# Scores of two heads on the two halves of the PE array, and an integer add in the weight decoder, in an attention and MLP kernel

## The chip, the cores and the metric

The kernel runs on one core of one Trainium2 chip. The metric is the device time of one execution in microseconds (us); lower is better. Five engines with a queue each work side by side: TensorE (PE, with its weight loads PEld), VectorE (DVE), ScalarE (ACT), GpSimd (POOL) and SyncE (SP), which here only issues DMAs. Each engine takes its instructions in the order in which the program has them.

## The reference: what is computed

```python
# q, k, v: 4 batches, 8 heads, 768 rows, head size 64; n_global = 8, n_local = 96
scores = q @ k.T / sqrt(64) + bias          # bias = -slope[head] * distance
scores = where(first 8 columns or the last 96 rows back, scores, -1e9)
x = softmax(scores) @ v                     # heads joined: 3072 tokens x 512
h = x @ w_in                                # 512 -> 2048, weights in float64
out = (h * clip(h + 3, 0, 6) / 6) @ w_out   # 2048 -> 512
```

## The kernel before, in words

The 3072 tokens are eight blocks of 384 (three tiles `t` of 128). A *pair* `n` is two neighbouring heads of one block, four pairs a block. For each pair and tile, `scores` multiplies the queries with a band of 232 keys (128 in the first tile of a batch), a DVE instruction adds the distances and takes the least ("weighing", L785), ACT takes the exponential and its sum (L789), `sum_up` and `normalize` divide (POOL for all pairs but the first), and `values` multiplies with V; `put_x` splits the result into a high and a low part, `xh` (ACT, L151) and `xl` (DVE, L152).

The first twelve pairs (`EARLY`, three blocks) go in plain float32: the normalized weights are turned by PE (`turn`, L815 and L817) and copied out by ACT (L819). For these, the queries of a pair lie in SBUF as two columns of 128 partitions, each with the other head's half zeroed, so that one matmul over all 128 partitions, with the keys of both heads stacked, gives the scores of one head. The other twenty pairs run in the fp32r format with split operands (`split`, L751 to L758) beside the MLP, in units of work that `attention` lays out.

The MLP runs in steps `f` of 128 hidden columns, sixteen a block: `first` (12 matmuls into `hp`, L165), the gate on ACT and DVE (`g`, L176 and L177), its high and low part (`gh`, `gl`), and `second` (9 matmuls into `acc`, L197). Weights arrive as float64 words in 32 chunks, two to a step. `decode` turns a chunk into two fp32r parts: ACT takes the magnitude (`wz`, L370), then DVE clamps (L389), shifts (L402), puts the sign back (L408), makes the exponent's value (L417), scales the low word by it (L392), adds (L406), and after ACT's rounding copy (L414) takes the rest (L399): seven DVE instructions of 128x512 a chunk. `fetch` loads a chunk into one of two buffers (`wst`).

Order: in the early stage a loop over `n` emits the scores of pair `n+2`, the turning of pair `n`, the sums of pair `n+1` and the values of pair `n-1`. A planner strews decoding steps and MLP steps between: `work(pe, dve)` books costs for PE and DVE, and while PE's account is ahead, the next decoding step is emitted; `decoded_to` forces steps that an MLP step needs. `LEAD` is the DVE account's start, `FIRST` the number of MLP steps of block 0 that go out within the early stage (after that, blocks 0 and 1 alternate, still with decoding). From pair 8 on (`self.more` false) the PSUM banks `acc` and `hp` belong to the MLP. PE, SP and POOL keep the order of emission; a scheduler places DVE's and ACT's instructions. `WAKE` idle matmuls open the program.

## Time and profile before

| | us |
|---|---|
| median of 3 runs | 675.01 (674.8 to 675.87) |
| the profiled execution, its own time | 674.91 |
| its span, first to last instruction | 673.0 |
| PE busy | 657.1 (98%) |
| DVE, ACT, POOL busy | 438.6, 282.9, 192.6 |

In a row of the timeline stand the start, the duration, the engine, the line, the operation, the tiles (written <- read), shapes and a count, and in brackets the time that the engine had been idle before and who ended that. Instructions of an engine overlap a little, so the distance from one start to the next (its *pitch*) is what an instruction costs the engine. A float32 matmul stands as two records.

### The profile page before, as it was taken

The numbers are of one execution on the slowest core, as the hardware profiler recorded it, in microseconds if no ns is written. First come the engines' busy times: TensorE is split into PE (matmuls) and PEld (weight loads), VectorE is DVE, ScalarE is ACT, GpSimd is POOL, SyncE is SP. The second block draws the span as 40 slices with busy tenths as digits, with TensorE's granted clock in tenths as the row PEclk, the third lists the DMA queues.
The fourth block names the chain that finished last, engine by engine and source line by source line (L and its number), as shares of the span: only waits on it lengthen the run. The fifth ranks groups of instructions, "written<-read, shape, count | busy, mean of one in ns | idle before, by whom it ended". The sixth has DMA issues, their size and how long they took to land.

```text
span 673.0 us, 11339 instructions
## 1 busy us (share of the span) xinstructions
PE 657.1 (98%) x3913; PEld 590.5 (88%) x3913; DVE 438.6 (65%) x1186; ACT 282.9 (42%) x744; POOL 192.6 (29%) x354
## 2 busy tenths in 40 slices
PE   7999899999999999999999999999999999999996
PEld 6788789999999889899989999899989999989995
DVE  8799899999975666457653676447762676422221
ACT  6899655554446333144333433143331443231111
POOL 2855400000000443233340343315431343302110
PEclk9999999999999999999999999999999999999999
DMA  8677432333303446524654367534555255510001
GB/s 255 176 230 242 146 124 100 121 110 110 97 29 133 131 135 181 158 94 132 165 140 119 103 172 189 147 94 126 138 160 141 79 150 142 141 47 2 1 1 52
DMA packets 62611, 84.33 MB, mean 125 GB/s; under 512 B 8784, under 2 KB 48720, under 8 KB 62544
## 3 DMA queue, kind: packets, MB, share of 16 engines
q1 hardware_dynamic: 62256, 83.25, 43.1%
q8 instruction: 33, 0.54, 0.3%
q14 instruction: 34, 0.28, 0.1%
q10 hardware_dynamic: 288, 0.26, 0.1%
HBM read 62.52 MB, written 20.97 MB: 124 GB/s over the span
## 4 chain that ended last, share of the span: by engine, by line
PE 84%; DMA 5%; ACT 4%; DVE 3%; issue 1%; POOL 1%; SPq 0%; POOLq 0%; ACTq 0%
PE hp L165 38%; PE acc L197 32%; DMA wst<-w 5%; ACT n L789 2%; PE sp L778 2%; PE xp L859 2%; PE tp L859 2%; PE sp L197 2%; PE tp L197 2%; PE xp L197 2%; PE tp L778 2%; POOL n L807 1%; ACT pt L819 1%; DVE n L785 1%; ACT wz L370 0%
## 5 line engine op out<-in xcount | busy, mean ns | idle before, releaser
L176 ACT ACTIVATE g<-hp,small 128x384 f32<-128x384 f32 x127 | 73.9, 582 | 256.0 <-PE hp L165 226.1
L165 PE MATMUL hp<-xh,w1h 128*128 128x384 f32 x512 | 174.0, 340 | 0.0
L165 PE MATMUL hp<-xh,w1l 128*128 128x384 f32 x512 | 172.8, 337 | 0.0
L165 PE MATMUL hp<-xl,w1h 128*128 128x384 f32 x512 | 171.9, 336 | 0.0
L183 POOL TENSOR_SCALAR gh<-g 128x384 fp32r<-128x384 f32 x96 | 57.8, 602 | 295.1 <-DVE g L177 265.2
L197 PE MATMUL acc<-w2h,gl 128*128 128x512 f32 x336 | 132.9, 396 | 0.1
L197 PE MATMUL acc<-w2l,gh 128*128 128x512 f32 x336 | 132.8, 395 | 0.0
L197 PE MATMUL acc<-w2h,gh 128*128 128x512 f32 x336 | 132.2, 393 | 0.0
L807 POOL TENSOR_SCALAR n<-n,sums 128x232 f32<-128x232 f32 (+1 forms) x186 | 104.9, 581 | 52.6 <-DVE sums L798 47.0
L177 DVE SCALAR_TENSOR_TENSOR g<-g,hp 128x384 f32<-128x384 f32 x128 | 70.2, 549 | 76.0 <-ACT g L176 75.4
L789 ACT ACTIVATE n<-n,least 128x232 f32<-128x232 f32 (+1 forms) x192 | 89.7, 471 | 40.3 <-DVE least L785 39.6
L190 DVE TENSOR_TENSOR gl<-g,gh 128x384 fp32r<-128x384 f32 x128 | 73.2, 572 | 45.7 <-POOL gh L183 44.0
L165 PEld LDWEIGHTS hp<-xh,w1h 128*128 128x128 f32 x512 | 96.3, 188 | 5.5 <-issue 1.5
L165 PEld LDWEIGHTS hp<-xl,w1h 128*128 128x128 f32 x512 | 96.2, 188 | 3.9
L165 PEld LDWEIGHTS hp<-xh,w1l 128*128 128x128 f32 x512 | 96.0, 188 | 0.0
L197 PEld LDWEIGHTS acc<-w2l,gh 128*128 128x128 f32 x336 | 63.0, 188 | 13.4
L197 PEld LDWEIGHTS acc<-w2h,gl 128*128 128x128 f32 x336 | 63.2, 188 | 11.8 <-DVE gl L190 1.5
L197 PEld LDWEIGHTS acc<-w2h,gh 128*128 128x128 f32 x336 | 63.3, 188 | 10.6 <-POOL gh L183 0.3
L832 DVE STREAM_TRANSPOSE blocks<-n 128x256 f32<-128x256 f32 x112 | 43.5, 424 | 27.1 <-POOL n L807 25.1
L752 POOL TENSOR_SCALAR kx<-load 64x504 fp32r<-64x504 f32 (+1 forms) x40 | 23.0, 575 | 119.0 <-PE hp L165 117.3
L785 DVE CUSTOM_DVE_ANT_0 n<-sp,d 128x232 f32<-128x232 f32 (+1 forms) x70 | 23.7, 376 | 36.8 <-PE sp L778 36.5
L789 ACT ACTIVATION_READ_ACCUMULATOR n<-n,least 128x1 f32 x192 | 36.9, 192 | 0.0
(113 smaller groups left out, 769.4 us busy)
## 6 DMA issues: line engine op xcount, KB each, us to landing
wst<-w SPq DMA_DIRECT2D x32, 512.0 KB, 3.5
there<-blocks SPq DMA_DIRECT2D x52, 256.0 KB, 2.6
load<-pairs SPq DMA_DIRECT2D x20, 636.0 KB, 5.2
load<-pairs SPq DMA_DIRECT2D x32, 384.0 KB, 4.0
weights<-there SPq DMA_DIRECT2D x48, 192.0 KB, 3.9
out<-o SPq DMA_DIRECT2D x23, 256.0 KB, 2.2
weights<-there SPq DMA_DIRECT2D x32, 160.0 KB, 3.3
load<-pairs SPq DMA_DIRECT2D x12, 252.0 KB, 4.7
```

The lines of the kernel that those rows point to most:

```text
L165: self.nc.tensor.matmul(hp, lhsT=self.w1(w, f)[:, kt, :], rhs=a[:, kt, :], start=(n == 0), stop=(n == 3 * NKT - 1))
L176: nc.scalar.activation(out=g, in_=hp, func=AF.Relu, bias=self.three, scale=1.0)
L177: nc.vector.scalar_tensor_tensor(out=g, in0=g, scalar=6.0, in1=hp, op0=ALU.min, op1=ALU.mult)
L183: self.nc.gpsimd.tensor_scalar(out=gh, in0=g, scalar1=1.0, scalar2=0.0, op0=ALU.mult, op1=ALU.add)
L190: self.nc.vector.tensor_tensor(out=gl, in0=g, in1=gh.bitcast(F32), op=ALU.subtract)
L197: self.nc.tensor.matmul(acc[tt], lhsT=a[:, tk], rhs=self.w2(w, f), start=(f == 0 and j == 0), stop=(f == NF - 1 and j == 2))
L778: nc.tensor.matmul(sp[:, j, lo:W], lhsT=q[:, t], rhs=part["kx"][:, c], start=(m == 0), stop=(m == 1))
L785: nc.vector.tensor_tensor_reduce(out=e[:, j, lo:W], in0=sp[:, j, lo:W], in1=d, op0=ALU.add, op1=ALU.min, scale=scale, scalar=3.0e38, accum ...
L789: nc.scalar.activation(out=e[:, j, lo:W], in_=e[:, j, lo:W], func=AF.Exp, bias=self.least[:, i:i + 1], scale=-1.0, accum_out=self.sums[:, ...
L807: nc.gpsimd.tensor_scalar(out=e[:, j, lo:W], in0=e[:, j, lo:W], scalar1=over, scalar2=0.0, op0=ALU.mult, op1=ALU.add)
L832: nc.vector.transpose(out=blocks[:, :, s].rearrange("p b j q -> p j b q"), in_=e[:, :, c:c + P].rearrange("p j (b q) -> p j b q", b=4))
L859: nc.tensor.matmul(xps[j * D:(j + 1) * D, t * P:(t + 1) * P], lhsT=vt[0:K, t, j * D:(j + 1) * D], rhs=self.part(t, j, c, K), start=(c == 0 ...
```

## The change

Four things change, beside line numbers.

1. For pairs 0 to 9 (`BOTH`) the queries are no longer padded with zeros: head `j` uses partitions `64j` to `64j+63` of queries and keys, and the two heads' matmuls go to two different PSUM banks. All three tiles' scores of a pair are emitted in one go, ahead of their weighing, and use four banks (`sp` and three of `acc`); `values` uses `xp` alone. The loads of a pair's keys and queries become one DMA, and the zeroing of the padding leaves DVE. Pairs 10 and 11 get their zeros by DMA.
2. In `decode` the exponent's value and the float add go. POOL turns the low word into an integer (`we`), and DVE adds it to the bit pattern with one 32-bit integer add, which the program has as an instruction over 128x1024 halfwords. DVE keeps five instructions a chunk. A chunk is fetched two ahead of its use rather than one, behind the third step.
3. For pairs 0 to 7 the second of three copies in `turn` goes from ACT to DVE. Two tiny mask steps go to POOL. Planner's costs, `LEAD`, `WAKE` and `FIRST` get other values.
4. In the later blocks the first step of `split` (ACT's `q1` and POOL's `kx`) is emitted ahead of the POOL normalizations of the same unit, no longer behind them.

```diff
+BOTH = 10
-LEAD = 5.0
-WAKE = 4
-FIRST = 5
+LEAD = 6
+WAKE = 7
+FIRST = 6
...
-        pools = {"s": (s, o, o), "t": (t, h, h), "x": (x, o)}[what] if self.more else {"s": (s, t)[:self.score_banks], "t": (t,), "x": (x,)}[what]
+        pools = {"s": (s, o, o, o), "t": (t, h, h), "x": (x,)}[what] if self.more else {"s": (s, t)[:self.score_banks], "t": (t,), "x": (x,)}[what]
...
-            parts = [(slice(KW + QW, LOAD), slice(None))] if values else [(slice(0, KW + QW), slice(None))]
-            if n < EARLY and not values:
-                parts = [(slice(0, KW), slice(None))] + [(slice(KW + j * TB, KW + (j + 1) * TB), slice(j * D, (j + 1) * D)) for j in range(2)]
-            for columns, rows in parts:
-                self.nc.sync.dma_start(out=self.place(n)[rows, columns], in_=self.pairs[n, rows, columns])
+            columns = slice(KW + QW, LOAD) if values else slice(0, KW + (TB if n < BOTH else QW))
+            self.nc.sync.dma_start(out=self.place(n)[:, columns], in_=self.pairs[n, :, columns])
...
     def magnitude(self, i):
+        words = self.raw[i].rearrange("p (c w) -> p c w", w=2)
+        self.e[i] = self.ep.tile([P, DM], I32, name="we")
+        self.nc.scalar.activation(out=self.z[i].bitcast(F32), in_=words[:, :, 1].bitcast(F32), func=AF.Abs)
+        self.nc.gpsimd.tensor_scalar(out=self.e[i], in0=words[:, :, 0].bitcast(U32), scalar1=2.0 ** -29, scalar2=0.0, op0=ALU.mult, op1=ALU.add)
...
-                stt(out=e, in0=words(i - 1)[:, :, 0].bitcast(U32), scalar=2.0 ** -52, in1=e, op0=ALU.mult, op1=ALU.mult)
-                if i + 1 < N:
-                    self.fetch(i + 1)
...
-                tt(out=e, in0=self.z.pop(i - 1).bitcast(F32), in1=e, op=ALU.add)
...
-                ts(out=self.e[i], in0=z, scalar1=-0x00800000, scalar2=None, op0=ALU.bitwise_and)
...
+                if i + 2 < N:
+                    self.fetch(i + 2)
+            yield 0.6 * a
+            if a:
+                tt(out=z, in0=z, in1=self.e.pop(i), op=ALU.add)
+                if i + 1 < N:
+                    self.magnitude(i + 1)
...
+                    if n + 2 < BOTH:
+                        weigh = [pairs[n + 2].scores(t) for t in range(NT)]
+                        self.load_next(n + 2, False)
+                        self.work(1.440, 0)
...
+            if after:
+                at[3].append(lambda after=after: after.split(0))
             at[3] += [me.sum_up, lambda me=me: me.normalize(0), lambda me=me: me.normalize(1)]
...
-            for t in range(NT if after else 0):
+            for t in range(1, NT if after else 0):
                 at[t + 3].append(lambda t=t, after=after: after.split(t))
...
+        sp = [self.banks[j][:, t % 2] if self.both else self.banks[0][:, j] for j in range(2)]
...
-                nc.tensor.matmul(sp[:, j, lo:W], lhsT=queries[:, j, t], rhs=keys[:, c], start=True, stop=True)
+                rows, q = (slice(j * D, (j + 1) * D), 0) if self.both else (slice(None), j)
+                nc.tensor.matmul(sp[j][:, lo:W], lhsT=queries[rows, q, t], rhs=keys[rows, c], start=True, stop=True)
...
-        nc.scalar.copy(out=pt[:, :, c], in_=tp[:, :, c])
+        (nc.vector.tensor_copy if kk.more and t == 1 else nc.scalar.copy)(out=pt[:, :, c], in_=tp[:, :, c])
```

How the order moves, at three places. First the early stage, one turn of the loop on PE; `load_72` and the like are the rooms of the pairs' data. Before, from the values of one pair on:

```order
L859 MATMUL xp<-pt,load_169 64x128 x10
L774 MATMUL acc<-load_169 128x232 x2
L815 MATMUL hp<-ident,n 128x128
L817 MATMUL hp<-ident,n 128x128
L815 MATMUL hp<-ident,n 128x128
L817 MATMUL hp<-ident,n 128x128
L774 MATMUL sp<-load_72 128x232 x2
L815 MATMUL tp<-ident,n 128x128
L817 MATMUL tp<-ident,n 128x128
L815 MATMUL tp<-ident,n 128x128
L817 MATMUL tp<-ident,n 128x128
L774 MATMUL acc<-load_72 128x232 x2
```

Now, from the scores of a pair to the values of the pair three before it:

```order
L773 MATMUL sp<-load_164 128x232
L773 MATMUL acc<-load_164 128x232
L773 MATMUL sp<-load_164 128x232
L773 MATMUL acc<-load_164 128x232 x3
L818 MATMUL tp<-ident,n 128x128 x2
L818 MATMUL hp<-ident,n 128x128
L820 MATMUL hp<-ident,n 128x128
L818 MATMUL hp<-ident,n 128x128
L820 MATMUL hp<-ident,n 128x128
L862 MATMUL xp<-pt,load_164 64x128 x10
```

Six matmuls a pair stay; they stand together, and neighbours write different banks. The same stage on ACT, from one `xh` to the next. Before:

```order
L151 CAST xh<-acc 128x384
L789 ACTIVATE n,sums<-n,least 128x232
L819 COPY pt<-hp 128x512
L789 ACTIVATE n,sums<-n,least 128x232 x2
L819 COPY pt<-tp 128x2x128
L789 ACTIVATE n,sums<-n,least 128x232 x2
L819 COPY pt<-hp 128x512
L789 ACTIVATE n,sums<-n,least 128x232 x2
L151 CAST xh<-xp 128x384
```

Now:

```order
L152 CAST xh<-xp 128x384
L822 COPY pt<-hp 128x512
L792 ACTIVATE n,sums<-n,least 128x232 x3
L822 COPY pt<-tp 128x2x128
L792 ACTIVATE n,sums<-n,least 128x232 x3
L152 CAST xh<-xp 128x384
```

One copy in three has left ACT. Second, the stretch in which blocks 0 and 1 alternate, on DVE, from one gate `g` to the next. Before:

```order
L177 SCALAR_TENSOR_TENSOR g<-g,hp 128x384
L408 SCALAR_TENSOR_TENSOR wz<-wst,wz 128x512
L399 TENSOR_TENSOR w1l_143<-we,w1h_142 128x4x128
L190 TENSOR_TENSOR gl<-g,gh 128x384
L417 TENSOR_SCALAR we<-wz 128x512
L389 TENSOR_SCALAR wz<-wz 128x512
L392 SCALAR_TENSOR_TENSOR we<-wst,we 128x512
L402 TENSOR_SCALAR wz<-wz 128x512
L406 TENSOR_TENSOR we<-wz,we 128x512
L177 SCALAR_TENSOR_TENSOR g<-g,hp 128x384
```

Now (L400 is the integer add):

```order
L178 SCALAR_TENSOR_TENSOR g<-g,hp 128x384
L400 ISA wz<-wz,we 128x1024
L385 TENSOR_SCALAR wz<-wz 128x512
L191 TENSOR_TENSOR gl<-g,gh 128x384
L386 TENSOR_SCALAR wz<-wz 128x512
L391 TENSOR_TENSOR w1l_1369<-wz,w1h_1368 128x4x128
L394 SCALAR_TENSOR_TENSOR wz<-wst,wz 128x512
L400 ISA wz<-wz,we 128x1024
L385 TENSOR_SCALAR wz<-wz 128x512
L178 SCALAR_TENSOR_TENSOR g<-g,hp 128x384
```

L417 and L392 are gone, and the float add has become the integer add, in place. Third, the later blocks on POOL, around one pair's normalizations. Before:

```order
L183 TENSOR_SCALAR gh<-g 128x384 x3
L807 TENSOR_SCALAR n<-n,sums 128x232 x4
L752 TENSOR_SCALAR kx<-load_73 64x504 x2
L807 TENSOR_SCALAR n<-n,sums 128x232 x2
L183 TENSOR_SCALAR gh<-g 128x384 x3
```

Now:

```order
L184 TENSOR_SCALAR gh<-g 128x384 x3
L748 TENSOR_SCALAR kx<-load_72 64x504 x2
L810 TENSOR_SCALAR n<-n,sums 128x232 x6
L184 TENSOR_SCALAR gh<-g 128x384 x3
L748 TENSOR_SCALAR kx<-load_73 64x504 x2
```

The two `kx` now stand ahead of all six normalizations.

More of the change, by code (lines that the diff above doesn't have):

```diff
@@ L409, in decode @@
[L409 to L411 removed]
+            yield 0.68 * a
             if b:
                 hi, sh = self.part(i - 1, self.w1h, self.w2h)
[L414 removed]
+                lo, _ = self.part(i - 1, self.w1l, self.w2l)
+                tt(out=lo, in0=sh(self.z.pop(i - 1).bitcast(F32)), in1=hi.bitcast(F32), op=ALU.subtract)
+            yield 0.6 * b
             if a:
[L416 to L417 removed]
```

102 lines of the change are left out of this document (44 added, 58 removed).

## The prediction

> **What bounds the kernel now.** I read the page's busy times first, then busy time by stage, then the timeline of the stage that changes.
>
> ```profile
> PE 657.1 (98%) x3913; PEld 590.5 (88%) x3913; DVE 438.6 (65%) x1186; ACT 282.9 (42%) x744; POOL 192.6 (29%) x354
> ```
>
> ```profile
> 0.00:20.00 20.00, 14.66 (x68) 11.93 (x68) 17.04 (x81) 13.18 (x47) 7.76 (x24) 1.00 0.85 248
> 20.00:56.00 36.00, 34.48 (x307) 29.85 (x305) 31.18 (x129) 34.21 (x114) 23.77 (x44) 1.00 0.72 214
> 56.00:97.00 41.00, 38.68 (x281) 34.13 (x282) 38.34 (x97) 28.40 (x72) 14.15 (x23) 1.00 0.51 160
> 97.00:206.00 109.00, 109.00 (x547) 98.62 (x546) 98.64 (x198) 54.24 (x97) 1.22 (x2) 1.00 0.28 92
> ```
>
> The columns are the stretch, its length, and the busy time of PE, PEld, DVE, ACT and POOL. Over the whole span PE is the bound, so PE work that goes is worth its time wherever no other engine then sets the pace. The stages differ: until 20 us DVE is the busiest, from 20 to 56 us PE (34.48 of 36) and ACT (34.21) are both full, from 56 to 97 us DVE is as full as PE, and from 97 to 206 us PE never stops while DVE is at 90%. The change touches all four.
>
> **The pairs on PE.** One pair of the early stage, with values, scores and turns between:
>
> ```profile
> 30.49 1.32 PE L859 MATMUL xp<-pt,load 128*64 128x128 f32 x20
> 31.74 1.05 PE L774 MATMUL acc<-load 128*128 128x232 f32 x4
> ...
> 33.06 0.95 PE L774 MATMUL sp<-load 128*128 128x232 f32 x4
> 33.85 0.27 PE L815 MATMUL tp<-ident,n 128*128 128x128 f32 x1
> ...
> 35.60 1.32 PE L859 MATMUL acc<-pt,load 128*64 128x128 f32 x20
> ...
> 43.51 0.61 PE L774 MATMUL sp<-load 128*128 128x128 f32 x4
> 43.95 0.27 PE L815 MATMUL tp<-ident,n 128*128 128x128 f32 x1
> ```
>
> From values to values it is 35.60 - 30.49 = 5.11 us. Two heads' scores cost 33.85 - 33.06 = 0.79 us at 232 columns and 43.95 - 43.51 = 0.44 us at 128. No row shows two matmuls on halves of the partitions. If they queue up, they cost what they cost now: 0.79. If they run at once, half: 0.40. The nearest row is the values, which use half the columns of the array for each head: ten matmuls of 128 columns would take 10 x 0.22 = 2.2 us one by one, and took 31.74 - 30.49 = 1.25. Two at a time gives 1.10, so 0.15 is left for going into that form and out. I take the half plus 0.15 a pair: 3 x 0.395 + 0.15 = 1.33 instead of 2.36, so 5.11 becomes 4.08. Over ten pairs (24 tiles of 0.79, six of 0.44: 21.6 us before, 10.8 + 1.5 after) 9.3 us of PE work go.
>
> The Trainium skill, "TensorEngine Tiling (Array Packing)", Key Properties, speaks against it: changing the tiling mode drains TensorE. It gives no figure; the values show such a change in and out within 0.15 us, so the trace agrees on its kind and holds it small; without it the PE sum would be 1.5 us better.
>
> **The pairs on ACT.** The stretch from the first `xh` to the first gate:
>
> ```profile
> 21.93 0.46 ACT L151 CAST xh<-xp 128x384 fp32r<-128x384 f32 x1
> ...
> 31.19 0.49 ACT L789 ACTIVATE n<-n,least 128x232 f32<-128x232 f32 x1
> ...
> 31.66 0.58 ACT L819 COPY pt<-hp 128x512 f32<-128x512 f32 x1
> 32.12 0.51 ACT L789 ACTIVATE n<-n,least 128x232 f32<-128x232 f32 x1
> ...
> 34.21 0.68 ACT L370 ACTIVATE wz<-wst 128x512 f32<-128x512 f32 x1 [0.65 <-DMA wst<-w]
> 34.78 0.57 ACT L819 COPY pt<-hp 128x512 f32<-128x512 f32 x1
> ...
> 42.50 0.62 ACT L414 CAST w1h<-we 128x512 fp32r<-128x512 f32 x1
> 43.02 0.50 ACT L789 ACTIVATE n<-n,least 128x232 f32<-128x232 f32 x1
> ...
> 59.33 0.61 ACT L176 ACTIVATE g<-hp,small 128x384 f32<-128x384 f32 x1
> ```
>
> Pitches: exponential 0.47, copy 0.46, magnitude 0.57, rounding copy 0.52. The stretch lasts 37.4 us. By the order, five exponentials fewer lie in it (38, not 43: the scores run further ahead, so they go before it), six copies fewer (now DVE's), two magnitudes and one rounding copy fewer. That is 5 x 0.47 + 6 x 0.46 + 2 x 0.57 + 0.52 = 6.8 us less ACT work. PE has seven pairs in it: 7 x 1.03 = 7.2 us less. DVE gets the copies (from PSUM, no row on DVE; between ACT's 0.46 and the 0.60 of a two-tensor operation of that size, below; I take 0.60) but loses decoding, and stays under both. So the stretch could fall by 6.8. Its work before adds up to about 35 us, so it ran 2 above; with PE, ACT and DVE now level I allow one more: **-5.8** (from -0.4 to -7).
>
> **The start.** DVE works from the arrival of the bounds to the first `xl` almost without a gap:
>
> ```profile
> 3.96 0.17 DVE L264 CAST fv<-iv 128x4 f32<-128x4 int32 x1
> ...
> 24.02 0.55 DVE L152 TENSOR_TENSOR xl<-xp,xh 128x384 fp32r<-128x384 f32 x1
> ...
> 71.02 0.38 DVE L785 CUSTOM_DVE_ANT_0 n<-sp,p 128x232 f32<-128x232 f32 x1
> ...
> 71.33 0.39 DVE L785 CUSTOM_DVE_ANT_0 n<-sp,p 128x232 f32<-128x232 f32 x1
> ...
> 95.49 0.43 DVE L389 TENSOR_SCALAR wz<-wz 128x512 f32<-128x512 f32 x1
> 95.83 0.69 DVE L392 SCALAR_TENSOR_TENSOR we<-wst,we 128x512 f32<-128x512 uint32 x1
> 96.43 0.55 DVE L177 SCALAR_TENSOR_TENSOR g<-g,hp 128x384 f32<-128x384 f32 x1
> 96.89 0.42 DVE L402 TENSOR_SCALAR wz<-wz 128x512 int32<-128x512 int32 x1
> 97.23 0.68 DVE L406 TENSOR_TENSOR we<-wz,we 128x512 f32<-128x512 f32 x1
> 97.83 0.68 DVE L408 SCALAR_TENSOR_TENSOR wz<-wst,wz 128x512 int32<-128x512 int32 x1
> ```
>
> Pitches: weighing 0.31, one-tensor operations of 512 words 0.34, two-tensor ones 0.60, those of 384 words (both gate parts, `xl`) 0.46. By the order, six decoding instructions leave this stretch (two of 0.34, four of 0.60: 3.1 us); two copies (1.2) and one weighing (0.3) come in: 1.6 us less. ACT however now has 24 exponentials there, not 19 (2.3 us more). I take **-1.5**, between 0 and -2. Three more idle matmuls (WAKE) run while PE waits for data and DVE for the masks: nothing. The zeroing on DVE ended before the bounds came: nothing. One DMA for three moves the same bytes: nothing; the first weight chunk is issued earlier.
>
> **Decoding.** A chunk loses 0.34 + 0.60 on DVE and the add changes form. No row has a 16-bit two-tensor operation. With two halfwords a step it costs the 0.60 of 512 words; with one, the slope from 384 words (0.46) to 512 (0.60) gives 0.60 + 512 x 0.14 / 128 = 1.16. I take 0.60, the row with the same bytes and streams; 1.16 is a rival. So a chunk costs 2 x 0.34 + 3 x 0.60 = 2.48 instead of 3.42.
>
> Block 1's first gate on ACT, and in the chain of waits the two halves of an MLP step:
>
> ```profile
> 95.35 0.58 ACT L176 ACTIVATE g<-hp,small 128x384 f32<-128x384 f32 x1
> ```
>
> ```profile
> 168.34 2.10 PE hp L165 x12
> 170.45 2.08 PE acc L197 x9
> ```
>
> A step takes 2.10 + 2.08 = 4.18 on PE. From the first gate to block 1's first, 36.0 us, DVE's order held 30.6 us at these pitches (decoding 20.9, gates 4.6, the rest of the pairs 5.1). Now one more MLP step lies in it (FIRST), which is PE work brought forward and no cost; and nine to ten chunks are decoded there, not six to seven, since at the first gate four are begun, not six: 23.0 + 5.5 + 5.8 = 34.3 us against 36.0 + 4.2 = 40.2. As free as before, but with less in reserve: **+0.8** (-2 to +3).
>
> After it DVE's order has 19 chunks (47.1) and 33 gate parts (15.2) on 17 gates: 62.3 us against 17 x 4.18 = 71.1 on PE. PE stays the bound, and less DVE work there is worth nothing: **0**.
>
> **POOL's new work.** A chunk gives POOL an instruction of 128x512 that it never had.
>
> ```profile
> 31.50 2.64 POOL L807 TENSOR_SCALAR n<-n,sums 128x232 f32<-128x232 f32 x6 [1.15 <-DVE sums L798]
> ...
> 77.55 5.08 POOL L807 TENSOR_SCALAR n<-n,sums 128x128 f32<-128x128 f32 x6 [6.73 <-DVE sums L798]
> ...
> 82.25 0.91 DVE L406 TENSOR_TENSOR we<-wz,we 128x512 f32<-128x512 f32 x1
> ...
> 222.16 1.30 POOL L752 TENSOR_SCALAR kx<-load 64x504 fp32r<-64x504 f32 x2
> ```
>
> Six normalizations take 2.64 us when DVE reads PSUM and 5.08 beside decoding; DVE's add is then stretched from 0.68 to 0.91, 0.23. By these rows POOL is the one that waits. A chunk's work on POOL lies between a `kx` of 504 words (1.30 / 2 = 0.65) and 0.97 (a normalization's 2.64 / 6 = 0.44, x 512 / 232). At 0.23 a chunk, DVE's 62.3 becomes 66.7 against 71.1 of PE: no cost.
>
> **The later blocks.** PE stalls there twice:
>
> ```profile
> L778 PE MATMUL sp<-kx,q 128*128 128x232 f32 (+1 forms) x140 | 21.2, 272 | 0.8 <-DVE kx L758 0.8
> ...
> L778 PE MATMUL tp<-kx,q 128*128 128x232 f32 (+1 forms) x100 | 15.3, 273 | 0.8 <-DVE kx L758 0.8
> ```
>
> DVE's `kx` follows POOL's, which stands behind four normalizations (about 2 us). Moved ahead, the 0.8 + 0.8 go; the normalizations come 1.3 us later, and their reader, the values, stands several MLP halves behind. **-1.5** (-1.7 to +1).
>
> **The sum.** -1.5 - 5.8 + 0.8 + 0 - 1.5 = -8.0 on the profiled execution's 674.9 gives 666.9; the median of the runs is 0.1 above it, so 667.0. Cross-check: that is 9.3 us less PE work, a little more PE waiting. The range of three runs before is 0.16%, so 0.2% (1.35 us) is what I count as a difference.
>
> **The rivals.**
> - *The halves queue up* (the change doesn't do what it says). PE keeps 5.11 a pair, the stretch gains 0.4: 674.9 - 0.4 - 1.5 + 0.8 - 1.5 + 0.1 = 672.4. Against it: the values run at once. 10%.
> - *The add takes a halfword a step.* 0.56 more a chunk: 5 us in the stretch from first gate to block 1 (39.3 of 40.2; perhaps 2 lost), 62.3 + 19 x 0.56 = 72.9 against 71.1 (1.8), four adds among the pairs (1): 671.7. 12%.
> - *POOL's new work holds DVE* (slower). If DVE stands still for x us a chunk, blocks 0 and 1 lose 19x - 8.8 (71.1 - 62.3) and the stretch before 9x - 3 (half of its 5.9 free us); together 28x - 11.8, and at 28x - 11.8 = 8.0, x = 0.71, the gain is gone. At x = 0.85, as long as a normalization beside decoding (5.08 / 6): +12.0, 679.0. For it: 0.71 lies within POOL's 0.65 to 0.97. Against it: 0.23 measured. 9%. The Trainium skill, "SBUF — State Buffer", "Who interferes with whom", has this rule: DVE and GpSimd share a port pair under an exclusive lock, and the one that comes second blocks fully. The trace agrees that they clash, and shows POOL bearing most of it.
> - *Waits between the engines hold the pairs.* A pair's scores need all four banks that the pair before it fills until it is weighed. If the pitch falls only to 4.9: -1.5 instead of -5.8, 671.3. 7%.
> - *Better:* the PE waits of the first 97 us (5.3, 1.5 and 2.3 us in the first three stretches) shrink by over half, since chunks are fetched earlier and ACT waits less for `wst`: 661.5. 9%.
>
> **Chances.** The forecast 53%, with its own range 663.5 to 670.5. Range of all: 661.5 to 673, which leaves out the slower rival and the tails of the others. Faster by over 0.2% (below 673.7): the forecast and nearly all of the four that stay below: 85%; within: 6%; slower: 9%.
>
> **What would show it.** Score records of the two heads starting together, 0.4 us a tile; a pair pitch of 4.3 to 4.6; the first gate near 52 instead of 59.3; the integer add at 0.6 to 0.7; PE without gaps from about 90 to 200 us; no wait of `q,kx` matmuls on `kx`. I am wrong if PE shows gaps between gates after block 1 has begun, if the add takes over 1.1, or if weighings wait for PE as much as they save.

## The result, and the profile after

The changed kernel takes 671.52 us (median of 5 runs, 671.4 to 672.34), the kernel before beside it 675.87: a ratio of 0.9944, 95% interval 0.9927 to 0.9962. The profiled executions took 671.40 and 674.91. So the gain is 3.5 us by the profiles, 3.8 by the ratio and 4.4 by the medians, where I forecast 8.0 (667.0). The sign was right, and the time lies in the wide range, 661.5 to 673; the forecast's own range, 663.5 to 670.5, does not hold it.

The page's busy times after, then the busy time by stage:

```profile
PE 654.7 (98%) x3919; PEld 584.1 (87%) x3919; DVE 424.3 (63%) x1121; ACT 278.4 (42%) x736; POOL 217.9 (33%) x389
```

```profile
0.00:20.00 20.00, 16.21 (x72) 12.24 (x72) 12.66 (x70) 12.33 (x45) 8.17 (x28) 1.00 0.73 249
20.00:56.00 36.00, 32.29 (x324) 26.26 (x323) 30.49 (x128) 32.24 (x114) 24.58 (x52) 1.00 0.77 225
56.00:97.00 41.00, 39.07 (x281) 33.99 (x280) 39.33 (x90) 29.64 (x71) 21.17 (x28) 1.00 0.57 181
97.00:206.00 109.00, 108.77 (x542) 97.33 (x541) 82.13 (x151) 52.63 (x94) 15.36 (x20) 1.00 0.27 87
```

PE lost only 2.4 us of busy time, not 9.3: between the points of the table below it lost 6.0 from pair 0's values to the first gate (31.5 for 37.5), but took 2.6 more ahead of them, where three more idle matmuls and a slower pace stand (last section), and 1.3 more in the two stages behind the first gate. From 20 to 56 us PE, DVE and ACT are all below 90% and none is full. From 56 to 97 DVE is fuller than PE. From 97 to 206 DVE fell from 98.6 to 82.1, and PE is no longer without a gap.

Where the time came from is read by following the same work through both traces. Rows of before: pair 0's values, then on ACT the gates 7, 32 and 127 (the last one on ACT), counted from the first gate of block 0:

```profile
20.09 1.32 PE L859 MATMUL xp<-pt,load 128*64 128x128 f32 x20
...
99.23 0.58 ACT L176 ACTIVATE g<-hp,small 128x384 f32<-128x384 f32 x1 [0.66 <-PE hp L165]
...
204.19 0.58 ACT L176 ACTIVATE g<-hp,small 128x384 f32<-128x384 f32 x1 [2.53 <-DVE gl L190]
...
659.25 0.58 ACT L176 ACTIVATE g<-hp,small 128x384 f32<-128x384 f32 x1 [3.60 <-PE hp L165]
```

After, the same and the first gate:

```profile
21.16 1.32 PE L862 MATMUL xp<-pt,load 128*64 128x128 f32 x20
...
56.34 0.57 ACT L177 ACTIVATE g<-hp,small 128x384 f32<-128x384 f32 x1
...
96.61 0.58 ACT L177 ACTIVATE g<-hp,small 128x384 f32<-128x384 f32 x1 [0.52 <-PE hp L166]
...
202.58 0.58 ACT L177 ACTIVATE g<-hp,small 128x384 f32<-128x384 f32 x1 [2.52 <-DVE gl L191]
...
655.66 0.58 ACT L177 ACTIVATE g<-hp,small 128x384 f32<-128x384 f32 x1 [3.60 <-PE hp L166]
```

| stage | forecast | measured (after less before, as it grows) |
|---|---|---|
| start to pair 0's values | -1.5 | 21.16 - 20.09 = **+1.07** |
| from there to the first gate | -5.8 | (56.34 - 59.33) - 1.07 = **-4.06** |
| first to 7th gate (block 1 begun in both) | +0.8 | -2.62 + 2.99 = **+0.37** |
| 7th to 32nd gate (blocks 0 and 1) | 0 | -1.61 + 2.62 = **+1.01** |
| 32nd to 127th gate (later blocks) | -1.5 | -3.59 + 1.61 = **-1.98** |

By this table 4.4 us are missing: 2.6 in the start, 1.7 in the pairs and 1.0 in blocks 0 and 1, less 0.9 by which the other two stages beat their forecast. Each column is one execution: g1_split_alone (below) has the order of before up to the 7th gate, and its trace took 0.6 longer from pair 0's values to the first gate and 1.4 longer from there to the 7th. So the second and third rows are good to about that; the fourth repeats within 0.04.

The prediction had drawn the first two stages between other points: the start on DVE, from the bounds' arrival to the first `xl`, and the pairs on ACT, from the first `xh` to the first gate. In its own stretches (length, then busy time of PE, PEld, DVE, ACT and POOL), the start before and after:

```profile
3.96:24.02 20.06, 16.46 (x93) 13.19 (x93) 17.56 (x86) 15.18 (x56) 9.96 (x21) 1.00 0.82 242
```

```profile
5.08:24.79 19.71, 17.49 (x104) 12.84 (x105) 15.65 (x84) 14.45 (x58) 10.95 (x28) 1.00 0.72 249
```

And the pairs:

```profile
21.93:59.33 37.40, 35.62 (x301) 31.19 (x300) 33.69 (x133) 36.03 (x123) 24.37 (x44) 1.00 0.77 233
```

```profile
24.23:56.34 32.11, 28.40 (x286) 23.19 (x283) 28.18 (x115) 29.54 (x104) 21.11 (x43) 1.00 0.80 237
```

By these the pairs are 37.40 - 32.11 = 5.29 shorter, nearly as forecast. The start is only 0.35 shorter and begins 1.12 later. And the two stretches overlap, by 2.09 us before and 0.56 after, so that 1.5 us in the sum of the two are counted twice. The first `xh` is 2.30 later, behind a wait of ACT for pair 3's weighing and that pair's exponentials:

```profile
21.11 0.40 ACT L792 ACTIVATE n<-n,least 128x128 f32<-128x128 f32 x1 [2.52 <-DVE least L788]
...
24.23 0.46 ACT L152 CAST xh<-xp 128x384 fp32r<-128x384 f32 x1
```

What the change says it does, it does. PE after, the scores of a pair, from one pair's values to the next:

```profile
25.36 1.32 PE L862 MATMUL xp<-pt,load 128*64 128x128 f32 x20
...
27.20 0.46 PE L773 MATMUL sp<-load 64*128 64x232 f32 x1
27.20 0.46 PE L773 MATMUL acc<-load 64*128 64x232 f32 x1
...
28.57 0.44 PE L818 MATMUL tp<-ident,n 128*128 128x128 f32 x2
...
29.94 1.32 PE L862 MATMUL xp<-pt,load 128*64 128x128 f32 x20 [0.49 <-DVE xl L153]
```

Both heads start in the same instant, and a pair's six scores take 28.57 - 27.20 = 1.37 us (forecast 1.33). The last row is new: PE stands 0.49 us before the values, since the bank `xp` is still read for `xl`. PE's waits from 20 to 58 us, with total, times and longest:

```profile
PE xp L862 <- DVE xl L153: 3.0, 5, 1.0
PE tp L818 <- ACT pt L822: 0.6, 2, 0.4
```

The integer add on DVE, with the next row's start 0.61 later (forecast 0.60):

```profile
33.00 0.69 DVE L400 CUSTOM_DVE_ANT_0 wz<-wz,we 128x1024 uint16<-128x1024 uint16 x1 [0.60 <-POOL we L367]
33.61 0.16 DVE L800 TENSOR_SCALAR sums<-sums 128x6 f32<-128x6 f32 x1
```

And in the later blocks the two waits for `kx` are gone (groups of the stretch from 206 us; the last figure is the idle time before):

```profile
L777 PE MATMUL sp<-kx,q 128*128 128x232 f32 x116 | 17.6, 273 | 0.0
L777 PE MATMUL tp<-kx,q 128*128 128x232 f32 x92 | 13.9, 273 | 0.0
```

### The profile page after: what moved, and what is told of

Same layout as the page of the kernel before. It is cut to its first block, busy times and chain, and to the rows that moved or that the text cites. A ratio compares the mean times of both kernels' runs of the same rounds, so it can differ in the third digit from the quotient of the medians.

```text
span 669.6 us, 11375 instructions
## 1 busy us (share of the span) xinstructions
PE 654.7 (98%) x3919; PEld 584.1 (87%) x3919; DVE 424.3 (63%) x1121; ACT 278.4 (42%) x736; POOL 217.9 (33%) x389
## 4 chain that ended last, share of the span: by engine, by line
PE 81%; DVE 7%; ACT 4%; DMA 3%; POOL 2%; issue 2%; POOLq 0%; ACTq 0%; SPq 0%; DVEq 0%
PE hp L166 36%; PE acc L198 33%; ACT n L792 3%; DMA wst<-w 2%; PE sp L777 2%; PE xp L862 2%; PE tp L862 2%; PE tp L777 2%; POOL n L810 1%; DVE wz L394 1%; DVE wz L400 1%; PE sp L198 1%; PE tp L198 1%; PE xp L198 1%; DVE wz L385 1%
## 5 line engine op out<-in xcount | busy, mean ns | idle before, releaser
L184 POOL TENSOR_SCALAR gh<-g 128x384 fp32r<-128x384 f32 x96 | 51.5, 537 | 294.0 <-DVE g L178 276.8
L810 POOL TENSOR_SCALAR n<-n,sums 128x232 f32<-128x232 f32 (+1 forms) x186 | 102.0, 564 | 36.6 <-DVE sums L801 17.5
L191 DVE TENSOR_TENSOR gl<-g,gh 128x384 fp32r<-128x384 f32 x128 | 79.4, 621 | 50.4 <-POOL gh L184 45.4
L835 DVE STREAM_TRANSPOSE blocks<-n 128x256 f32<-128x256 f32 x112 | 43.5, 424 | 29.2 <-POOL n L810 18.7
L367 POOL TENSOR_SCALAR we<-wst 128x512 int32<-128x512 uint32 x32 | 25.5, 797 | 70.3 <-DMA wst<-w 63.2
L748 POOL TENSOR_SCALAR kx<-load 64x504 fp32r<-64x504 f32 (+1 forms) x40 | 31.1, 778 | 37.8 <-PE hp L166 36.2
```

What stands on the lines that cost most here:

```text
L184: self.nc.gpsimd.tensor_scalar(out=gh, in0=g, scalar1=1.0, scalar2=0.0, op0=ALU.mult, op1=ALU.add)
L191: self.nc.vector.tensor_tensor(out=gl, in0=g, in1=gh.bitcast(F32), op=ALU.subtract)
L748: nc.gpsimd.tensor_scalar(out=part["kx"][own, c], in0=k[own, c], scalar1=1.0, scalar2=0.0, op0=ALU.mult, op1=ALU.add)
L810: nc.gpsimd.tensor_scalar(out=e[:, j, lo:W], in0=e[:, j, lo:W], scalar1=over, scalar2=0.0, op0=ALU.mult, op1=ALU.add)
L835: nc.vector.transpose(out=blocks[:, :, s].rearrange("p b j q -> p j b q"), in_=e[:, :, c:c + P].rearrange("p j (b q) -> p j b q", b=4))
```

## The experiments

Every kernel was timed in five rounds beside the kernel before (675.0 to 675.4 in these groups); ratios are to that. Unless said otherwise an edit is made on the changed kernel, and times are to be held against its 671.5 (0.9944).

### The start

The rows after that show it: the bounds arrive at 5.08 (3.96 before), the first weighing starts at 7.45 (5.81 before), and DVE then stands almost 2 us for pair 3's distances, which POOL makes behind pair 1's normalizations.

```profile
5.08 0.17 DVE L265 CAST fv<-iv 128x4 f32<-128x4 int32 x1 [4.21 <-DMA iv<-bounds]
...
7.45 0.29 DVE L788 CUSTOM_DVE_ANT_0 n<-sp,p 128x128 f32<-128x128 f32 x1 [0.72 <-ACT p L317]
...
20.77 0.29 DVE L788 CUSTOM_DVE_ANT_0 n<-sp,p 128x128 f32<-128x128 f32 x1 [1.92 <-POOL p L319]
```

**e1_bounds_first.**
```diff
-        nc.scalar.dma_start(out=self.iv, in_=self.bounds.broadcast_to([P, 4]))
+        nc.sync.dma_start(out=self.iv, in_=self.bounds.broadcast_to([P, 4]))
```


> Changed kernel (671.4 in its profile) with one edit: the small load of the two bounds is issued first on SyncE's queue, ahead of the pairs' loads, and no longer on ScalarE's. Theory S (the start lost what is missing, and what the start loses stays lost): the bounds' cast on DVE moves from 5.08 to about 4, the first weighing from 7.45 to about 6.4, the values of pair 0 from 21.16 to about 20.2, and the time falls by 0.8 (0.4 to 1.1), to 670.6. Theory V (the pairs are held by the one bank of the values, where PE waits 3.0 us for xl, whatever the start does): the first weighing moves, but the first gate does not by more than 0.3 from 56.34, and the time stays within 0.4 of 671.4.

Measured 671.19 (0.9942, 0.993 to 0.9955): no difference. The bounds came at 3.53 and pair 0's values at 19.03, 2.1 earlier, but pair 1's at 24.46, 0.9 earlier, after the same wait for pair 3's distances; the first gate was 1.0 earlier and the 7th 0.33.

**e2_dist_early.**
```diff
-                    if n + 2 < NPAIR:
-                        self.distances(n + 2)
+                    for m in {-2: (0,), -1: (1,), 0: (2, 3)}.get(n, ()):
+                        self.distances(m)
```


> Changed kernel with one edit: the four distance products of pair 3 stand on POOL ahead of pair 1's six normalizations, no longer behind them. Theory S: DVE's wait of 1.92 for p at 20.77 goes, ACT's wait of 2.5 at 21.11 shrinks, values from pair 1 on come 1 us earlier, the first gate near 55.3, the time 0.6 to 1.2 lower, 670.5. Rival: POOL is late by as much elsewhere (pair 1's normalizations, on which PE's transposes wait, come 1.6 later), and the time stays within 0.4 of 671.4, or rises by up to 0.8.

Measured 671.20 (0.994, 0.9927 to 0.9953): no difference. The wait went, but pair 0's values came at 22.04, and by pair 4 (39.91 against 40.04) nothing was left. Each repair alone leaves the other delay standing.

**e4_warm.**
```diff
-WAKE = 7
+WAKE = 10
```


> Changed kernel with one edit: ten idle matmuls at the start, not seven, so that PE is busy without a gap until the first scores. In the changed kernel a transpose takes 0.21 until 20 us and 0.11 after; before the change it was 0.11 from 14 us on. If three more idle matmuls close the gap, PE's fast pace begins before 9 us and not at 20 (transposes at 15 to 17.5 with 0.11 a piece, six 64x232 scores of a pair in 1.4 and not 2.3). Theory S: the values of pair 0 then come 0.5 to 1 earlier and the time falls by 0.3 to 0.8, to 670.9. Theory V: PE waits for data in the start anyway, and the time stays within 0.3 of 671.4. If the transposes still take 0.21, the slow pace does not hang on that gap.

Measured 672.72 (0.9964, 0.9951 to 0.9977), 1.2 slower. PE was at its fast pace by 6.5 us, but the granted clock then fell to 0.50 from 13 to 23 us; pair 0's values came 1.0 late, of which 0.6 is left at the first gate (56.91) and at the last (656.28). Neither theory's time holds.

**h1_full_start.** Scores of pairs 0 to 3 over the whole array:
```diff
+FULL = 4
...
-                rows, q = (slice(j * D, (j + 1) * D), 0) if self.both else (slice(None), j)
+                rows, q = (slice(j * D, (j + 1) * D), 0) if self.both and self.n >= FULL else (slice(None), j)
```


> Changed kernel, but the scores of pairs 0 to 3 are matmuls over all 128 partitions (padded queries, 196 KB more to load for each), those of pairs 4 to 9 on half the array as in the changed kernel. Theory H (in the first 20 us matmuls on half the array do not bring PE to its fast pace: it is at 0.21 a transpose until 20.5 us in the changed kernel and at 0.11 from 8.9 us on with padded queries): transposes at 14 to 17 take 0.11, pair 0's values come near 19.8 and not 21.16, pair 7's near 55.6, and the time falls by 0.8 to 1.5, to 670.3. Rival W (the 1.3 us are lost again where DVE waits for POOL's distances of pair 3 at 20.4): pair 1's values at 25 as now, the time within 0.4 of 671.5.

Measured 672.18 (0.9948, 0.9935 to 0.9961): no gain. PE was fast before 10 us (its scores of pair 1 begin at 9.29 slow and end at 11.58 fast), pair 0's values came at 20.45, pair 1's at 25.89: rival W, though the time is 0.7 above the changed kernel's. PE's pace in the start is real, and not what sets the time.

**f2_first5_start.** Both repairs of the start, and `FIRST = 5`.

> Changed kernel with three edits: five MLP steps of block 0 in the early stage, the bounds' load issued first on SyncE, and pair 3's distance products ahead of pair 1's normalizations on POOL. The first run of the bounds alone had pair 0's values 2.1 us earlier, the first gate 1.0 earlier and block 1's first gate only 0.33 earlier. Theory R: what the start gains is lost between the first gate and block 1's because DVE's decoding is the bound there; with one step fewer in that stretch the 1.0 stays, and the time falls by 0.8 to 1.8, to 670.2. Rival: the earlier start is eaten in the pairs (PE's waits for xl) and in PE's slow pace in the first 20 us; then within 0.4 of f1.

Measured 670.17 (0.9924, 0.9905 to 0.9943); its profiled execution 669.05. Pair 0's values and the first gate in it:

```profile
19.04 1.21 PE L862 MATMUL xp<-pt,load 128*64 128x128 f32 x18
...
53.71 0.58 ACT L177 ACTIVATE g<-hp,small 128x384 f32<-128x384 f32 x1
```

Pair 0's values are 2.1 earlier, the first gate 2.6, and its 127th gate (653.17) 2.5: in this trace the whole gain of the start reaches the end. It is the fastest of the six executions; by the medians 1.4 us are gained. **f1_first5** (`FIRST = 5` alone) shows that the one step fewer gains nothing by itself: 671.85 (0.995, 0.9932 to 0.9968).

> Changed kernel with five MLP steps of block 0 inside the early stage, as before the change, not six. Theory R (DVE is the bound from the first gate to block 1's: 39.3 us busy of 41, and PE waits there for a decoded chunk, w1h, 0.3 us; six steps need twelve chunks by then, five need ten): PE's waits in 56 to 97 us (1.9) fall under 1.2, and the time falls by 0.3 to 1, to 670.9. Theory N (a step brought forward costs nothing, as I forecast): within 0.3 of 671.4, either way.

So theory N of that run holds (0.3 above the changed kernel), and R falls as far as the number of steps goes. **h2_full_bounds_dist** (h1 and both repairs, with six steps) was the fastest kernel of all.

> The kernel of h1 with two more edits: the bounds' load first on SyncE, and pair 3's distances ahead of pair 1's normalizations on POOL. Theory H and the start as the cause together: pair 0's values near 18.3, pair 7's near 53.5, time 2.5 to 3.5 under the changed kernel, 668.5. If the pace of PE matters no more once bounds and distances are early, the same as with those two edits and five steps (670.2, pair 0's values at 19.04, pair 7's at 54.38). If the pairs' stretch takes up what the start gains, 670.5 to 671.5.

Measured 669.34 (0.9918, 0.9902 to 0.9935). Its first gate stands at 53.84, that of f2 at 53.71, so PE's pace again gave nothing that the trace shows. With the start mended the change is worth 5.1 (f2) and 5.5 us (h2) by the ratios, where it was worth 3.8. So by ratios and medians the start was a third to a half of what was missing; by the profiled executions (669.05 and 668.71 against 671.40) it was over half.

### The pairs

**e3_two_x.**
```diff
-        pools = {"s": (s, o, o, o), "t": (t, h, h), "x": (x,)}...
+        pools = {"s": (s, o, o, o), "t": (t, h), "x": (x, h)}...
```


> Changed kernel with one edit: the values of the early pairs take turns between two banks (xp and hp), and the turns have two (tp and hp) where they had three. Theory V: PE's waits for xl (3.0 us in five places) go, the pairs' mean pitch falls from 4.9 to about 4.5, the first gate from 56.34 to about 54, the time by 1.5 to 3, to 669. Theory S: the waits for xl turn into waits elsewhere in the same pair (for turns, or for weighings), since DVE and ACT hold the pitch; the pitch stays at 4.8 to 5.0, the time within 0.5 of 671.4.

Measured 672.77 (0.9969, 0.9955 to 0.9983), slower by 1.2. The waits for `xl` went and came back in front of the transposes:

```profile
PE tp L818 <- ACT pt L822: 3.1, 2, 1.6
```

From pair 0's to pair 7's values it took 35.9 us, as in the changed kernel (35.8). Theory V falls: the wait is where PE happens to meet the pace of the others. That is theory S, but the time lies outside its 0.5.

**e6_padded.** The two heads one after another over all partitions, everything else as changed but for the queries' longer loads:
```diff
-                rows, q = (slice(j * D, (j + 1) * D), 0) if self.both else (slice(None), j)
+                rows, q = slice(None), j
...
```


> Changed kernel with the two heads' matmuls over all 128 partitions again (queries padded with zeros, as before the change; the loads of pairs 0 to 9 are 196 KB longer), in the new order and into the new banks. So PE gets back 0.4 us a tile of 232 columns, some 1 us a pair, and nothing else changes. Theory M (the half-array matmuls carry the gain): from pair 0's values to pair 7's it takes 40 to 42.5 us and not 35.8, the time rises by 3 to 6, to about 675.5, no faster than before the change. Theory D (DVE and ACT hold the pairs, and the gain is from decoding): PE's waits for xl (3.0) vanish instead, the stretch takes 36 to 38, and the time rises by at most 1.5, to 673.

Measured 672.96 (0.9965, 0.995 to 0.998): the half-array matmuls are worth 1.4 us, not 6. The stretch took 37.3 us, against 35.8 with them and 39.8 before. But its pair 0's values came at 19.83, 1.3 earlier (PE's pace, see the last section), and its pair 1's at 25.26, 0.1 earlier, after the same wait for pair 3's distances (1.5 here). From pair 1's to pair 7's values it took 31.8 us, with half-array matmuls 31.6, before the change 34.3: of these 2.7 us only 0.3 are theirs. At the last gate the two traces differ by 0.4; the profiled execution (671.99) is the fastest of its ten. PE has no room left in this run: from the first `xh` to the first gate it is busy for 32.3 of 32.6 us. Theory D, at the upper end of its price.

**e7_copy_act.**
```diff
-        (nc.vector.tensor_copy if kk.more and t == 1 else nc.scalar.copy)(...)
+        nc.scalar.copy(...)
```


> Changed kernel with all three copies of a turn on ACT again (DVE has none). It moves seven copies from DVE (0.6 each) to ACT (0.46 each). If ACT holds the pairs' pitch, pair 0's to pair 7's values take 35.8 + 2 to 3.2, and the time rises by as much, to 674. If DVE holds it, the stretch falls by 1 to 3, and the time with it, to 670. If neither does alone, but each waits for the other in turn (sums for exponentials, exponentials for weighings), the time stays within 1 of 671.5.

Measured 673.31 (0.9973, 0.9958 to 0.9988): 1.8 slower. The stage from 20 to 56 us:

```profile
20.00:56.00 36.00, 31.09 (x318) 25.25 (x317) 25.11 (x118) 33.84 (x116) 24.07 (x51) 0.98 0.73 208
```

DVE drops to 25.1, ACT rises to 33.8: ACT holds the pairs more than DVE or PE does, as I had reckoned. From the first `xh` to the first gate ACT has 2.4 us more to do, and takes 1.1 longer; pair 0's to pair 7's values take 36.5, 0.8 longer and not 2 to 3.2, so that the time fits none of the three cases. In the changed kernel ACT waits 1.7 us here for weighings, beside the one of 2.5 in the start, and DVE 2.8 for exponentials ahead of the sums; the rest of the pitch is this turn-taking, which no run took away.

### The decoding

**d1_decode_alone.** The kernel before, with the new `magnitude` and `decode` and nothing else of the change.

> Kernel before the change with the new decoding alone (integer add, the low word on POOL, a chunk fetched two ahead; two heads one after another, copies on ACT). From the changed kernel's trace: blocks 0 and 1 lose about 1.0 (PE's second halves take 2.2 to 2.6 in four places where gl comes late, and 2.08 before), since DVE's add waits for POOL's part. In the pairs ACT and PE keep their work, so DVE's relief gives 0 to 1.5 there. Sum: 674.0 to 676.0, taken 675. If DVE's relief carries the gain of the pairs, as the padded run suggests (its stretch from pair 0's to pair 7's values took 37.3 and not 39.8), 672.5 to 673.5. My forecast for decoding was 0 in blocks 0 and 1, and nothing by itself in the pairs: 675.

Measured 677.46 (1.0031, 1.0019 to 1.0044): slower by 2.3. It lost 1.65 from the first to the 7th gate, which is little over the scatter there (1.4), and 1.15 from the 7th to the 32nd. Neither of the expected ranges (674.0 to 676.0, 672.5 to 673.5) holds it.

**k4_alone_no_low** and **k2_no_low.** The same, and the changed kernel, without POOL's instruction:
```diff
-        self.nc.gpsimd.tensor_scalar(out=self.e[i], in0=words[:, :, 0].bitcast(U32), ...)
...
-                tt(out=z, in0=z, in1=self.e.pop(i), op=ALU.add)
+                tt(out=z, in0=z, in1=self.nought, op=ALU.add)
```


> Kernel before the change with the new decoding alone, and of that without POOL's instruction (zeros are added). With it: 677.5. Theory P: the 2.3 us go, and with two DVE instructions fewer a chunk it comes to 674 to 675.1. Rival O: 676.5 to 677.5.

> Changed kernel without POOL's new instruction (the 32 conversions of the low words are left out; the integer add stays in its place and adds a tile of zeros, so the last bits of the weights are missing). Theory P (POOL's part is what decoding costs: it stretches DVE's instructions beside it, and the add waits for it, and gl behind the add): blocks 0 and 1 lose their 1.0 us of longer second halves (all 2.07 to 2.13), the stretch from first gate to block 1's is 0.5 to 1.5 shorter, the time 1.5 to 2.5 lower, 669.5. Rival O (the place of decoding in DVE's order costs it, or the load of chunks two ahead): within 0.5 of 671.5.

Measured 676.02 (1.0015, 1.0 to 1.003) alone, and 671.84 (0.9944, 0.9927 to 0.9961) in the changed kernel. Alone it falls between the two theories: POOL's part is 1.1 (by the ratios) to 1.4 of the 2.3 us, and what the rest is stays open. By the total, k2 says that POOL's part costs nothing. By stage it says something else: from the 7th to the 32nd gate PE loses 0.01 us (1.01 with POOL's part), and alone 0.01 (1.15). What k2 gains there it lost in the start: DVE's adds came earlier there, POOL's six normalizations took 4.17 instead of 3.07 beside them, and pair 3's weighing stood until 22.43. How POOL's part costs, from DVE's groups between 100 and 200 us (busy, mean ns of one; idle before). Changed kernel:

```profile
L400 DVE CUSTOM_DVE_ANT_0 wz<-wz,we 128x1024 uint16<-128x1024 uint16 x19 | 16.4, 861 | 0.4
L191 DVE TENSOR_TENSOR gl<-g,gh 128x384 fp32r<-128x384 f32 x23 | 14.0, 611 | 4.1 <-ACT gh L186 4.1
```

Without POOL's part:

```profile
L193 DVE TENSOR_TENSOR gl<-g,gh 128x384 fp32r<-128x384 f32 x24 | 13.3, 553 | 4.1 <-ACT gh L188 4.1
...
L400 DVE CUSTOM_DVE_ANT_0 wz<-wz,nought 128x1024 uint16<-128x1024 uint16 x19 | 13.0, 685 | 0.1
```

The add is 0.18 longer and `gl` 0.06, about 0.25 us a chunk on average. Single instructions show how: three of the 23 `gl` take 1.01 us and the others about 0.55, and these three begin while POOL converts a chunk. The first of them, and POOL's instruction:

```profile
120.80 1.01 DVE L191 TENSOR_TENSOR gl<-g,gh 128x384 fp32r<-128x384 f32 x1
```

```profile
120.73 0.67 POOL L367 TENSOR_SCALAR we<-wst 128x512 int32<-128x512 uint32 x1 [2.74 <-DMA wst<-w]
```

Half of the adds take 0.76 to 1.15, the others 0.68 or 0.69. DVE has the room (82 of 109 us), but four `gl` come late, and PE, which needs them at once, stretches four second halves; one of them in the chain, beside a plain one:

```profile
134.98 2.08 PE acc L198 x9
143.37 2.20 PE acc L198 x9
```

**m5_three.**
```diff
-            self.decoding(words, 2, 2, side="right")
+            self.decoding(words, 3, 2, side="right")
```


> Changed kernel with three buffers for the weight chunks (wst), not two; the order of all instructions is the same, only a chunk's load need no longer wait for the chunk before last. Theory L (in blocks 0 and 1 POOL's and ACT's parts of a chunk start when its load lands, which is when DVE's add and gl stand there; earlier chunks take them apart): the four longer second halves (2.19 to 2.59) come to 2.08, PE loses nothing from the 7th to the 32nd gate (1.0 now), PE's wait for w1h (0.3) goes, time 0.8 to 1.5 lower, 670.4. Rival: POOL's part costs the same wherever it stands beside DVE, or the earlier chunk loads delay the pairs' loads: within 0.4 of 671.5, or above.

Measured 672.19 (0.9956, 0.9941 to 0.9971): theory L falls. POOL's part now meets other instructions. Between 100 and 200 us the add is back at its length and `gl` stretched instead:

```profile
L191 DVE TENSOR_TENSOR gl<-g,gh 128x384 fp32r<-128x384 f32 x24 | 16.9, 706 | 4.1 <-ACT gh L186 4.1
...
L400 DVE CUSTOM_DVE_ANT_0 wz<-wz,we 128x1024 uint16<-128x1024 uint16 x19 | 13.0, 682 | 0.4
```

It moves the cost and does not remove it. Blocks 0 and 1 lose 0.6 rather than 1.0, but at 84 us POOL's conversion stands ahead of the normalizations, and PE's transposes wait 1.6 for it. **m2_three** (h2 with three buffers) agrees: 669.70 (0.9922, 0.9905 to 0.9939), no better than h2.

> The kernel of h2 (full-array scores for pairs 0 to 3, the bounds' load first, pair 3's distances early; 669.3) with three chunk buffers. Theory L: 668.2 (667.5 to 669). Rival: 669.3 or more.

**k1_old_decode.** The changed kernel with the old `magnitude` and `decode`.

> Changed kernel with the decoding of before (seven DVE instructions a chunk, float add, nothing of it on POOL, a chunk fetched one ahead); the heads side by side, the copies on DVE and all else as changed. Theory Q (the new decoding by itself costs time wherever it stands: alone on the kernel before it made 677.5 of 675.1): 2 to 2.5 us less than the changed kernel, 669.3. Theory A (the changed kernel has the DVE copies and so needs the shorter decoding; the old one makes DVE the bound from 25 to 97 us): 1 to 4 us more, 674.

Measured 684.4 (1.013, 1.0109 to 1.0152): 12.9 slower. Nearly all of it falls between the second and the 6th gate, where PE waits for decoded weights:

```profile
PE hp L166 <- ACT w1h L407: 5.1, 2, 3.8
PE hp L166 <- DVE w1l L392: 1.4, 2, 1.0
```

Theory A, three times its highest price; **k3_old_decode_start** is the same on h2 and says the same, 687.46 (1.0171, 1.0149 to 1.0193).

> Changed kernel with the old decoding, and with the three edits of h2 (full-array scores for pairs 0 to 3, the bounds' load first, pair 3's distances ahead of pair 1's normalizations), which made 669.3. Theory Q: the two add, 667.0 (666 to 668). Theory A: 670 to 673.

So the decoding costs 2.3 us alone and is worth 12.9 inside the change: it makes room on DVE for the copies and for twelve chunks by the 6th gate, which the kernel before did not ask for. The planner's costs, `LEAD` and `FIRST` stay those of the new decoding in both runs; with values of their own they might lose less, which no run shows.

### The later blocks

**g1_split_alone.** The kernel before, with `split(0)` ahead of the normalizations.

> Kernel before the change with one part of it alone: in the later blocks the first step of the split is emitted ahead of the normalizations. My forecast for this part was -1.5 (0.8 + 0.8 of PE's waits for kx go): 673.4. From the traces the later blocks gave 0.9 (from block 1's first gate to the end): then 674.0. If the two waits come back in another place (PE waits for q or for values), 674.9.

Measured 673.14 (0.9967, 0.9952 to 0.9983): 2.1 less. In its trace the 32nd to the 127th gate take 1.98 less than before, exactly as in the changed kernel. (The profiled execution is one of its slowest, 675.29; what it lost lies ahead of the 7th gate.)

## Why the prediction was right or wrong, point by point

- **The bound.** PE's own saving was sized well where PE runs fast (a pair's scores 1.37, from 20 to 56 us 9.8 us of score records for 18.7), but PE was not what set the pairs' pace: padded matmuls (e6) fill PE again and give back 1.4 us only. "PE work that goes is worth its time wherever no other engine then sets the pace" was true, and another engine did.
- **The start: this step failed.** Forecast was -1.5; by the prediction's own end, the first `xl`, it is 24.79 - 24.02 = +0.77, at pair 0's values +1.07, and at ACT's first `xh` +2.30. The sum of DVE's work was right: 17.6 us before, 15.7 after, 1.9 less where 1.6 was counted. What failed is that DVE would go on working "almost without a gap" from a fixed start: it stands 4.1 us in this stretch, 2.5 before, and begins 1.1 later. I put "one DMA for three moves the same bytes" and the two mask steps on POOL at nothing. The bounds land 1.1 later, behind the loads issued beside them; issued first they land early (e1). Whether the one larger DMA a pair does it, or the first weight chunk, which SyncE now issues at 1.65 us and not at 4.21, no run separates. From the bounds to the first weighing it takes 2.37 us, 1.85 before, with the steps on POOL in that chain; no run took them back. And I did not look at POOL's queue, where pair 3's distances wait behind pair 1's normalizations; the trace of before had that wait already (1.18). f2 took away the late bounds and that wait: its first `xh` comes at 21.10, 0.8 earlier than before the change, and 2.5 us reached the end of its trace (1.4 by the medians).
- **The pairs: -5.8 against -5.29 by the prediction's own ends, right.** The table has -4.06, since it starts at pair 0's values and so has the late first `xh` in it. The mechanism, ACT's work, was right: 6.5 us less of it where 6.8 was counted, and 1.2 us more of waiting where one was allowed; with the copies back (e7) the stretch grows by under half of what ACT gets back. What was wrong is the joint with the start: a start that ends at the first `xl` (24.02) and pairs that begin at the first `xh` (21.93) cannot simply be added. The pitch came to 4.9, from 5.2, and not to 4.3 to 4.6. I had a pitch of 4.9 as a rival at 7%, by the banks of scores and with 1.5 us off the stretch; the pitch came, the small gain did not. From 20 to 58 us PE waits for none of them (list above), and e3 shows that the bank of the values does not hold the pairs either.
- **First gate to block 1: +0.8 against +0.37**, inside its range, with a scatter larger than the difference. That a sixth step costs nothing is shown by f1 and h2. That DVE has "less in reserve" is shown by k1.
- **Blocks 0 and 1: 0 against +1.01, wrong.** The sum was right: the add at 0.61, 0.25 a chunk for POOL (I took 0.23), DVE far from full. The test was wrong. I asked whether DVE's total stays under PE's; PE does not wait for a total but for `gl`, and one `gl` that is late by 0.2 costs 0.2. I had written that gaps between gates after block 1 has begun would prove me wrong, and they are there.
- **POOL holding DVE** as a slower rival had the right mechanism at under a third of its size (0.25 us a chunk, where it took 0.85). By its own sum, 19x - 8.8, that would cost blocks 0 and 1 nothing; the cost came through single late `gl`. The Trainium skill, "SBUF — State Buffer", "Who interferes with whom", has the second comer block fully. The trace agrees for single instructions: each of the three long `gl` ends 0.41 to 0.43 us after the conversion that it met. m5 shows which DVE instruction is hit change with the moment, and the mean stretch is 0.06 to 0.18 us, since not every one meets POOL's.
- **The later blocks: -1.5 against -1.98**, right; the normalizations that now come later delayed nobody.

What stays open: which parts of the change shorten the pairs. From pair 1's to pair 7's values 2.7 us went; the half-array matmuls are 0.3 of them (e6) and the copies 0.9 (e7), and the old decoding makes this stretch no longer (k1, 30.4 against 31.6). The new order, in which a pair's scores stand ahead of its weighing, was not taken back by a run. The turn-taking of DVE and ACT (about 0.4 us a pair over my forecast) was read from waits and not taken away either.

## What to carry to other kernels

Before a stage's work is summed between two ends, ask what the change does to the ends, and let neighbouring stretches share them: a few bytes that everything waits for can fall behind other loads, and a delay that is mended alone may only uncover the next one. An engine with room to spare still delays a full one through a single late instruction, so check latency where the bound engine waits, not only totals. Parts of a change can be worth the opposite of what they do alone: measure them out of the whole as well as into the kernel before.

## What the runs showed of the hardware

PE's pace in the first 20 us. In the changed kernel a transpose takes 0.21 us until 20 us, and half that right after; in the run with padded queries it has the short pitch at 14 us. The changed kernel, then the padded run:

```profile
15.43 0.42 PE L820 MATMUL hp<-ident,n 128*128 128x128 f32 x1
15.64 0.42 PE L818 MATMUL hp<-ident,n 128*128 128x128 f32 x1
...
20.73 0.27 PE L820 MATMUL hp<-ident,n 128*128 128x128 f32 x1
20.84 0.27 PE L818 MATMUL hp<-ident,n 128*128 128x128 f32 x1
```

```profile
13.83 0.27 PE L818 MATMUL hp<-ident,n 128*128 128x128 f32 x1
13.94 0.27 PE L820 MATMUL hp<-ident,n 128*128 128x128 f32 x1
```

The page of the changed kernel has a granted clock of 1.00 all along, which cannot be so: m5, with the same order and the same busy times, has 0.50 for that stretch. From 8 to 20 us, the changed kernel and m5:

```profile
8.00:20.00 12.00, 10.51 (x46) 7.57 (x46) 10.71 (x61) 9.84 (x40) 4.44 (x12) 1.00 0.70 252
```

```profile
8.00:20.00 12.00, 10.58 (x46) 7.58 (x46) 10.64 (x61) 9.81 (x40) 4.45 (x12) 0.50 0.69 253
```

So the column is to be read with the pitch of a known instruction beside it. The Trainium skill, "TensorE: Matmul & The Clock Gate", "What's actually happening", has PE at half its clock until it has been busy for about 3.4 us on end. The padded run agrees (busy from 5.2, fast by 8.9). In the changed kernel PE was busy 10.5 of the 12 us from 8 to 20 and stayed slow, which that rule does not say (from 8 to 14 it was busy for 5.7 of 6 us). h1, with the full array in pairs 0 to 3, was fast before 10 us; but e1 and f2, with half-array scores, were slow from about 7.5 and fast again by 14.4. That half-array matmuls count for less there is what these runs suggest, and no run measured it by itself.
